# A third PSUM bank for the attention scores, and fewer exponentials in PSUM

## The chip, the cores and the metric

One core of a Trainium2 chip runs the whole kernel. The metric is the device time of one execution in microseconds; the median of several runs is compared. TensorE (PE) multiplies, VectorE (DVE) and ScalarE (ACT) read and write both SBUF and the eight PSUM banks, GpSimd (POOL) works on SBUF, and SyncE (SP) issues the transfers. Each engine executes its own instructions strictly in the order in which the program issues them; between engines, semaphores order producers, consumers and the reuse of buffers.

## The reference

A transformer block with adaptive layer norm. Sequence 2048, width 512, 32 query heads and 8 key/value heads of 128, the last 512 keys of a cache, then a gated feed-forward layer of width 1792. All inputs are f32.

```python
mod = (silu(c) @ w_mod).reshape(1, 6, 1, 512)          # shift, scale and gate, twice
h = layernorm(x) * (1 + ca) + sa
q = h @ wq                                             # (2048, 32 x 128)
p = softmax(q @ k^T * 128**-0.5)                       # over 512 keys, per head
x = x + ga * ((p @ v) @ wo)
h = layernorm(x) * (1 + cb) + sb
x = x + gb * ((gelu(h @ w_gate) * (h @ w_up)) @ w_down)
```

## The kernel before

Every f32 product is made of three f16 products: each operand is split into a high half and a residual, `high` and `low`, and `mm3` (lines 87 to 91) issues low x high, high x high and high x low into one PSUM bank. With f16 halves, a group of three matmuls of 128x128 by 512 columns is the unit of PE work everywhere.

The attention is cut into 128 **units**: one head and one block of 512 queries. A unit has four **slots**, each of 128 queries against all 512 keys, so there are 512 slots, counted by `t`; slot `t` belongs to unit `t // 4`. The main loop (lines 1564 to 1609) issues for each slot, in this order:

- `scores(t)` (line 979): one `mm3` group into a bank called `ps`;
- `peak(t)` (line 988): on DVE, the negated row maximum `nm` of that bank;
- the DVE halves of whatever projection or value product ended in the slot before (`split_post`, line 746: ACT writes the high half, DVE the residual; tiles `qt`, `ot`, and some weights `w`, `k`);
- the reciprocals `rr` of two slots' row sums (line 1002), each second slot;
- `low(t - 3)` (line 1014): on DVE, the f16 residual of the probabilities, from the exponentials `ee`, the factor `rr` and the high half; then, on SP, a transposing DMA of the slot's high half and residual into the tile `pt`;
- `expo(t)` (line 993): on ACT, the exponential of the scores into `ee` with its row sum;
- `high(t - 2)` (line 1009): on ACT, the high half of the probabilities;
- up to three groups from the queue `work` (line 1507, `pop`), with the steps that follow them. In the stretch of the change these are the next unit's query projection (`q_plain`, line 921: four groups into a bank `pq`) and the value product of the unit two before (`pv_tasks`, line 935: four groups into `po`). A value product reads all four transposed slots of its unit. From slot 30 on, groups of the output projection (`y_tasks`, line 948, bank `py`) join them.

So in slots 12 to 29 a unit has 36 matmuls, and the fourth slot of a unit pops nothing; later a unit has 48.

POOL meanwhile scales and splits weights and keys (lines 155 to 163), and makes the sums and differences of activations (line 582) for a seven-product scheme that replaces `q_plain` from unit 12 on (`q_items`, line 898; first issued near slot 42).

PSUM has eight banks under three names. `s` (two banks) holds scores, in turn. `acc` (five banks) is handed out in turn to everything that accumulates: `pq`, `po`, `py`, small reductions (`pst`, `prow`). `qa` (one bank) is used at the start for matmuls that keep PE running and for one small product (slots 2 to 9), and again by `q_items`. A tile that takes a bank waits until the last reader of the bank's former tile is done.

The table `PSE` (line 56) names the slots whose exponentials `ee` go to a PSUM bank, and which one: 13 slots take an `acc` bank and 5 the `qa` bank. All other slots write `ee` to one of six SBUF buffers (`tmp`, line 75). In both cases `high` and `low` read `ee` from where it lies; `low` also reads the high half, which is in SBUF, and writes to SBUF.

## Time and profile before

| what | value |
|---|---|
| runs, median (lowest to highest of 3) | 1733.12 us (1732.55 to 1733.29) |
| the profiled execution | 1734.19 us |
| its span, first to last instruction | 1732.4 us |
| PE busy | 1711.2 us, 99% of the span |
| DVE busy | 1425.8 us, 82% |
| ACT busy | 1254.3 us, 72% |
| POOL busy | 1093.3 us, 63% |
| `ee` on ACT, 512 times | 349.6 us, mean 683 ns |
| residual `low` on DVE, 512 times | 454.1 us, mean 887 ns |
| transposing DMA, 512 times | 3.5 us from issue to landing, median |

A busy PE in this table is not a PE at its peak: matmuls overlap, and a matmul's row is longer than the distance to the next one. Times in the timelines count from the start of the span. An instruction's row also overlaps the next row of its engine a little, so the time that it holds its engine is read from start to start. In a timeline, a bracket gives the idle time of the engine before the row and what ended it. In the groups the names stand as `out<-in`, and line 91 is that of `mm3`, whatever called it.

### The profile page before, as it was taken

To read this page: it belongs to the slowest core of one execution; us is meant where nothing else is said; L and a number is where in the kernel's file an instruction comes from. 1 tells how busy PE (TensorE), PEld (TensorE's weight loads), DVE (VectorE), ACT (ScalarE), POOL (GpSimd) and SP (SyncE) were. 2 spreads that over 40 slices of the span, in tenths; PEclk is the share of its full clock that TensorE was granted. 3 is DMA by queue.
4 is the path that set the end of the run, shared out by engine and by line. 5 is a ranking of instruction groups with operands and counts; after the bars stand their busy time and mean duration, and the time that the engine had idled before them with its cause. 6 is when DMAs were issued, how large, how long until landed. Compare 5 with 4: busy or idle time off the path is not lost.

```text
span 1732.4 us, 26343 instructions
## 1 busy us (share of the span) xinstructions
PE 1711.2 (99%) x8012; PEld 787.1 (45%) x8012; DVE 1425.8 (82%) x2476; ACT 1254.3 (72%) x2819; POOL 1093.3 (63%) x1328
## 2 busy tenths in 40 slices
PE   7999999999999999999999999999999999999998
PEld 5444444444444444444444444444444444444444
DVE  7888898988888899888888888888896788676666
ACT  6988788888888777897787777787785354455442
POOL 4879778777788884655665755747760345735424
PEclk9999999999999999999999999999999999999999
DMA  7999999999999998999999999999997556355353
GB/s 234 218 208 210 214 214 205 225 205 220 211 229 222 206 210 181 219 207 224 198 232 219 206 231 208 203 218 221 229 227 164 163 145 196 118 164 174 96 157 104
DMA packets 693454, 343.51 MB, mean 198 GB/s; under 512 B 579136, under 2 KB 602688, under 8 KB 693312
## 3 DMA queue, kind: packets, MB, share of 16 engines
q1 hardware_dynamic: 693024, 341.30, 85.4%
q8 instruction: 63, 1.03, 0.3%
q14 instruction: 79, 0.65, 0.1%
q10 hardware_dynamic: 288, 0.52, 0.1%
HBM read 137.50 MB, written 63.70 MB: 116 GB/s over the span
## 4 chain that ended last, share of the span: by engine, by line
PE 86%; DVE 5%; ACT 4%; POOL 2%; DMA 2%; issue 1%; SPq 0%; POOLq 0%; DVEq 0%; ACTq 0%
PE py L91 18%; PE po L91 17%; PE ps L91 16%; PE fa L91 8%; PE qa L91 8%; PE fc L91 4%; PE qc L91 4%; PE ya L91 3%; PE fb L91 2%; PE qb L91 2%; PE yc L91 2%; ACT ee L999 1%; DVE p L1016 1%; DVE nm L990 1%; ACT p L1011 1%
## 5 line engine op out<-in xcount | busy, mean ns | idle before, releaser
L999 ACT ACTIVATE ee<-ps,nm 128x512 f32<-128x512 f32 x512 | 349.6, 683 | 184.2 <-DVE nm L990 181.0
L1016 DVE SCALAR_TENSOR_TENSOR p<-ee,rr,p 128x512 f16<-128x512 f32 x512 | 454.1, 887 | 8.1 <-ACT p L1011 7.5
L990 DVE TENSOR_REDUCE nm<-ps 128x1 f32<-128x512 f32 x512 | 350.3, 684 | 105.7 <-PE ps L91 102.9
L91 PE MATMUL ps<-k,qt 128*128 128x512 f16 x1536 | 414.9, 379 | 3.8 <-ACT ee L999 2.5
L1011 ACT ACTIVATE p<-ee,rr 128x512 f16<-128x512 f32 x512 | 363.9, 711 | 21.9 <-DMA pt<-p 11.6
L91 PE MATMUL po<-pt,v 128*128 128x512 f16 x1536 | 372.9, 379 | 2.8 <-DVE kmax L184 1.0
L91 PE MATMUL py<-wo,ot 128*128 128x512 f16 x1536 | 371.3, 379 | 0.0
L91 PEld LDWEIGHTS <-w 128*128 128x128 f16 x2184 | 214.0, 98 | 259.7 <-issue 2.7
L91 PEld LDWEIGHTS <-v 128*128 128x128 f16 x1536 | 149.9, 98 | 185.1 <-issue 5.1
L91 PEld LDWEIGHTS <-ot 128*128 128x128 f16 x1536 | 150.3, 98 | 181.2
L91 PEld LDWEIGHTS <-qt 128*128 128x128 f16 x1536 | 145.8, 98 | 174.8 <-issue 3.3
L1320 POOL TENSOR_TENSOR fg<-fg 128x512 f32<-128x512 f32 x48 | 63.0, 1312 | 147.0 <-DVE fg L1294 144.2
L748 DVE SCALAR_TENSOR_TENSOR ot<-po,ot 128x512 f16<-128x512 f32 x128 | 87.8, 686 | 37.7 <-ACT ot L747 37.3
L1304 ACT ACTIVATE at<-fg 128x512 f16<-128x512 f32 x92 | 56.3, 626 | 80.1 <-DVE fg L1294 61.7
L999 ACT ACTIVATION_READ_ACCUMULATOR ee<-ps,nm 128x1 f32 x512 | 100.1, 195 | 0.0
L960 DVE SCALAR_TENSOR_TENSOR acc<-py,ysc,acc 128x512 f32<-128x512 f32 x128 | 94.7, 740 | 5.3 <-PE py L91 5.3
L91 PE MATMUL qa<-t,w 128*128 128x512 f16 x348 | 84.9, 379 | 0.0
L236 POOL TENSOR_TENSOR lw<-lw,half__86 128x1 f32<-128x1 f32 x39 | 25.0, 641 | 91.0 <-DVE lw L186 91.0
L91 PE MATMUL fa<-t,w 128*128 128x512 f16 x336 | 81.7, 379 | 0.1
L747 ACT ACTIVATE ot<-po 128x512 f16<-128x512 f32 x128 | 73.9, 577 | 5.0 <-PE po L91 5.0
L403 POOL TENSOR_TENSOR rs<-rs,nhalf 128x1 f32<-128x1 f32 x32 | 18.7, 586 | 92.9 <-DVE rs L397 90.0
L91 PEld LDWEIGHTS <-wo 128*128 128x128 f16 x504 | 49.3, 98 | 60.6 <-issue 1.3
(243 smaller groups left out, 2821.9 us busy)
## 6 DMA issues: line engine op xcount, KB each, us to landing
w<-kept SPq DMA_DIRECT2D x123, 256.0 KB, 3.3
wo<-kept SPq DMA_DIRECT2D x72, 256.0 KB, 3.3
kept<-stage SPq DMA_DIRECT2D x67, 256.0 KB, 3.2
raw<-in_wo SPq DMA_DIRECT2D x56, 256.0 KB, 3.2
kept<-w SPq DMA_DIRECT2D x39, 256.0 KB, 3.3
rw<-in_wq SPq DMA_DIRECT2D x38, 256.0 KB, 3.1
hs<-hf SPq DMA_DIRECT2D x32, 256.0 KB, 2.8
pt<-p SPq DMA_TRANSPOSE x512, 3.5
```

Of the source, the lines that this page charges most:

```text
L91: nc.tensor.matmul(ps, a, b, start=first and n == 0, stop=last and n == 2, skip_group_check=chain)
L236: nc.gpsimd.tensor_tensor(out, out, half_, op=ALU.pow)
L403: nc.gpsimd.tensor_tensor(st["rs"], st["rs"], nhalf, op=ALU.pow)
L747: nc.scalar.activation(t[:, 0, :], src, AF.Copy, scale=scale)
L748: return lambda: nc.vector.scalar_tensor_tensor(t[:, 1, :], src, scale, t[:, 0, :], op0=ALU.mult, op1=ALU.subtract)
L960: nc.vector.scalar_tensor_tensor(acc[ti], st["p"], by, acc[ti], op0=ALU.mult, op1=ALU.add)
L990: nc.vector.tensor_reduce(nm, E[t]["ps"], axis=AX.X, op=ALU.max, negate=True)
L999: nc.scalar.activation(e, E[t]["ps"], AF.Exp, bias=E[t]["nm"], scale=1.0, accum_out=sm[:, t % 2:t % 2 + 1])
L1011: nc.scalar.activation(p16[:, 0, :], E[t]["e"], AF.Copy, scale=E[t]["r"])
L1016: nc.vector.scalar_tensor_tensor(p16[:, 1, :], E[t]["e"], E[t]["r"], p16[:, 0, :], op0=ALU.mult, op1=ALU.subtract)
L1304: nc.scalar.activation(t[:, 0, :], g, AF.Copy)
L1320: nc.gpsimd.tensor_tensor(g[o], g[a], g[b], op=ALU.subtract)
```

## The change

```diff
-PSE = dict.fromkeys((5, 7, 8, 9, 14, 18, 19, 21, 22, 23, 25, 26, 27), "acc") | dict.fromkeys((11, 15, 20, 24, 28), "qa")
+PSE = dict.fromkeys((5, 6, 10, 14, 18, 19, 20, 22, 23, 24, 26, 27, 28), "acc")
...
     def scores(t):
...
-        ps = bank("s", "ps", 2)
+        ps = bank("qa", "ps", 1) if 12 <= t < 40 and t % 3 == 2 else bank("s", "ps", 2)
```

Two things change. The scores of slots 14, 17, 20, 23, 26, 29, 32, 35 and 38 go into the `qa` bank; the slots between them share the two `s` banks in turn as before, so that from slot 14 to about slot 40 a score bank is taken again three slots later and not two. And the `qa` bank is no longer used for exponentials: the table names 13 slots, all with `acc` banks. Against the table before, slots 7, 8, 9, 11, 15, 21 and 25 go from PSUM to SBUF, slots 6 and 10 from SBUF to PSUM, and slots 20, 24 and 28 from the `qa` bank to an `acc` bank. No instruction is added or removed, and the order of instructions on each engine stays as it was.

## The prediction

> **What bounds the kernel now.** I read the page first, then busy time by stretch, then the chain of waits inside the stretch that the diff touches, then the timelines of that stretch engine by engine.

> ```profile
> span 1732.4 us, 26343 instructions
> ...
> PE 86%; DVE 5%; ACT 4%; POOL 2%; DMA 2%; issue 1%; SPq 0%; POOLq 0%; DVEq 0%; ACTq 0%
> ...
> pt<-p SPq DMA_TRANSPOSE x512, 3.5
> ```

> TensorE holds 86% of the chain. Slots 5 to 40 fall between 39 and 125 us. Busy time there, in three stretches:

> ```profile
> 25.00:52.80 27.80, 26.60 (x146) 14.62 (x147) 23.41 (x49) 22.89 (x56) 15.88 (x25) 1.00 0.80 183
> 52.80:97.00 44.20, 40.21 (x178) 17.30 (x176) 38.74 (x71) 40.12 (x99) 34.72 (x44) 0.96 1.01 215
> 97.00:130.00 33.00, 32.94 (x156) 15.04 (x157) 27.78 (x52) 26.70 (x63) 24.20 (x35) 1.00 0.93 209
> ```

> Columns: stretch, length, then busy time of PE, weight loads, DVE, ACT, POOL, then the granted clock. After 97 us PE idles 0.06 us in 33. In the 44.2 us before, PE idles 4, ACT 4.1 and DVE 5.5. So whatever the change does must be done before 97 us, and a shift of that moment goes through to the end. The chain of waits there begins and ends so:

> ```profile
> 52.11 0.68 PE ps L91 x3
> ...
> 97.06 1.46 PE po L91 x6
> ```

> Every piece between these two lines is DVE, ACT or issue time; PE does not appear once. PE's own waits there: in the first line those of score groups for exponentials (total, times, longest), then rows of the timeline (in brackets: idle before the row and what ended it):

> ```profile
> PE ps L91 <- ACT ee L999: 2.4, 3, 1.9
> ```
> ```profile
> 60.22 1.46 PE L91 MATMUL po<-pt,v 128*128 128x512 f16 x6 [0.65 <-DVE ysc L234]
> ...
> 82.82 0.95 PE L91 MATMUL ps<-k,qt 128*128 128x512 f16 x3 [1.86 <-ACT ee L999]
> 83.57 2.77 PE L91 MATMUL pq<-y,w 128*128 128x512 f16 x6
> ...
> 93.05 2.10 PE L91 MATMUL pq<-b,w 128*128 128x512 f16 x9
> ...
> 97.06 1.46 PE L91 MATMUL po<-pt,v 128*128 128x512 f16 x6 [0.61 <-DVE nm L990]
> ```

> The three score groups (slots 20, 23, 24; the last at 82.82) found their bank still read by the exponential of two slots before. The wait at 97.06 is put down to `nm`, which the value product does not need. What it needs is the transposed tile of slot 23, last of its unit:

> ```profile
> 91.53 0.75 DVE L748 SCALAR_TENSOR_TENSOR qt<-pq,qsc,qt 128x512 f16<-128x512 f32 x1 [0.24 <-ACT qt L747]
> 92.20 0.15 DVE L1007 RECIPROCAL rr<-rr 128x2 f32<-128x2 f32 x1
> 92.27 0.73 DVE L1016 SCALAR_TENSOR_TENSOR p<-ee,rr,p 128x512 f16<-128x512 f32 x1
> ```
> ```profile
> 93.06 1.23 SPq L1020 DMA_TRANSPOSE pt<-p  x1
> ```

> The residual ends at 93.00, SP issues the transpose at 93.06, and with the page's median of 3.5 us it lands near 96.6; I take the landing as the releaser. So before 97 us the pace is that of DVE and ACT handing slots to one another, and PE waits for slot 23.

> **The third score bank.** No instruction is added. Nine score groups change bank; each score group of slots 14 to 40 then waits for the exponential three slots back, not two. That takes away the 2.4 us of PE idling (1.86 of it at 82.82), and the slow matmuls behind the longest (rows at 82.82 and 83.57). What is late next?

> ```profile
> 81.53 0.75 DVE L748 SCALAR_TENSOR_TENSOR qt<-pq,qsc,qt 128x512 f16<-128x512 f32 x1 [0.98 <-ACT qt L747]
> ```

> Slot 24 opens unit 6, whose queries' low half this row writes until 82.28; the third score matmul reads it. So this group gains at most 0.4 us. The projection behind it (83.57) takes the accumulator bank five tiles back, the last unit's projection, which the same row reads: it cannot start before 82.28 either. PE's next value product needs slot 19, whose residual ended at 83.00, and after it comes the wait of 97.06. PE time won here is handed back in front of these. I price the bank at 0, covered by the landing of slot 23. Bounds: -0.4 (if the residuals follow the scores a little) to 0.

> **The exponentials.** 18 PSUM destinations become 13: slots 7, 8, 9, 11, 15, 21 and 25 go to SBUF, 6 and 10 to PSUM; 20, 24 and 28 only change from the q bank to the accumulators. Two instructions per moved slot change their source: ACT's `high` and DVE's `low`.

> ```profile
> 56.51 0.67 ACT L1011 ACTIVATE p<-ee,rr 128x512 f16<-128x512 f32 x1
> 57.08 0.59 ACT L152 ACTIVATE gate<-prow 128x512 f32<-128x512 f32 x1
> ...
> 59.69 0.71 ACT L1011 ACTIVATE p<-ee,rr 128x512 f16<-128x512 f32 x1
> 60.31 0.62 ACT L219 ACTIVATE junk<-raw 128x512 f16<-128x512 f32 x1
> ```

> Slot 9 (PSUM) holds ACT 0.57 us to the next start, slot 10 (SBUF) 0.62. On the chain are slots 9, 11, 15 and 21, and slot 10 the other way: (4 - 1) x 0.05 = +0.15 us.

> DVE's residual is the larger term:

> ```profile
> 54.16 0.73 DVE L1016 SCALAR_TENSOR_TENSOR p<-ee,rr,p 128x512 f16<-128x512 f32 x1
> ...
> 56.09 0.74 DVE L1016 SCALAR_TENSOR_TENSOR p<-ee,rr,p 128x512 f16<-128x512 f32 x1
> 57.70 0.69 DVE L192 TENSOR_REDUCE gam<-gate 128x1 f32<-128x512 f32 x1 [0.87 <-ACT gate L152]
> ...
> 63.84 0.73 DVE L1016 SCALAR_TENSOR_TENSOR p<-ee,rr,p 128x512 f16<-128x512 f32 x1
> 64.49 0.68 DVE L990 TENSOR_REDUCE nm<-ps 128x1 f32<-128x512 f32 x1
> 65.48 0.69 DVE L748 SCALAR_TENSOR_TENSOR ot<-po,ot 128x512 f16<-128x512 f32 x1 [0.30 <-ACT ot L747]
> ...
> 74.33 1.42 DVE L1016 SCALAR_TENSOR_TENSOR p<-ee,rr,p 128x512 f16<-128x512 f32 x1
> ...
> 86.59 0.72 DVE L1016 SCALAR_TENSOR_TENSOR p<-ee,rr,p 128x512 f16<-128x512 f32 x1
> 87.95 0.69 DVE L990 TENSOR_REDUCE nm<-ps 128x1 f32<-128x512 f32 x1 [0.64 <-PE ps L91]
> ```
> ```profile
> 50.64 0.92 POOL L159 TENSOR_SCALAR w<-rw 128x512 f16<-128x512 f32 x1
> ...
> 53.56 0.62 POOL L159 TENSOR_SCALAR w<-rw 128x512 f16<-128x512 f32 x1
> 54.27 1.15 POOL L160 TENSOR_TENSOR w<-rw,w 128x512 f16<-128x512 f32 x1
> ...
> 63.35 1.27 POOL L582 TENSOR_TENSOR u<-cb,u 128x512 f32<-128x512 f32 x1
> ...
> 73.94 1.26 POOL L657 TENSOR_TENSOR wor<-wor,gs 128x512 f32<-128x512 f32 x1
> ```

> Slot 16 (74.33, SBUF) started inside a POOL pass that ended at 75.20 and itself ended at 75.75, 0.55 later, after 1.42 us. Slot 11 (63.84, PSUM) lay inside a POOL pass too and took 0.73. Bounds for a moved slot: 0 (POOL idle or behind) to +0.7.

> [...]

> Slot by slot. *Slot 7*: slot 6, now read from PSUM, no longer slows the POOL pass at 50.64 (0.92 against 0.62), so POOL runs 0.3 us earlier and its add of 54.27 spans 53.97 to 55.12. Slot 7's residual at 54.16 falls inside: it ends at 55.12 + 0.55 = 55.67, not 54.89, **+0.78**. The next maximum, its exponential, ACT's `gate` (57.08) and DVE's wait of 0.87 us for it all queue behind, so it stays. *Slot 8* (56.09): taken as blocked too, but DVE waits 0.87 us for the gate behind it, and that wait covers up to 0.7: 0. *Slots 9, 15 and 25*: POOL's timeline shows it idle or in one-column operations there: 0. *Slot 11*: inside the pass 63.35 to 64.62, ends 65.17 in place of 64.57; the maximum behind it then runs 65.09 to 65.70, past the 65.48 at which the next row starts today after waiting 0.30 for ACT: **+0.22** on the chain. *Slot 21* (86.59): blocked by at most 0.7, with the 0.64 behind it (87.95) as cover; if the third bank removes that wait, the next cover is DVE's wait for ACT at 91.53: 0. Sum: 0.78 + 0.15 + 0.22 = 1.15, say **+1.2 us** on slot 23's residual, its landing, 97.06, and the end.

> The profiled execution took 1734.19 us (1.8 around its span); the median of the runs is 1733.12, 1.07 lower. So 1735.4 for a profile and **1734.3 us** for the median. A measurement of this kernel tells 0.2%, 3.5 us, from no change; the forecast lies within.

> **The rivals.** *The score banks were the limit (faster).* If slot 23 follows the scores, the 2.4 us go, and with them the slow clock:

> ```profile
> 81.00:82.80 1.80, 0.00 (x0) 0.10 (x1) 1.27 (x3) 1.80 (x5) 1.72 (x3) 1.00 0.23 50
> 82.80:86.20 3.40, 3.38 (x10) 1.27 (x10) 3.40 (x6) 2.44 (x6) 3.22 (x4) 0.58 1.17 307
> ```

> After 1.86 us of idling the granted clock averaged 0.58 over 3.4 us, and six matmuls took 2.77 us (83.57) against 1.46 (60.22): 3.4 x (1 - 1.46 / 2.77) = 1.6 us lost. Time: 1733.1 - 2.4 - 1.6 = 1729.1. For it: the waits are there. Against it: the chain holds no PE piece, and ACT is busy 40.1 us of 44.2.

> *The wait ahead of slot 29's value product lowers the clock (slower).* That wait (97.06) grows. The projection at 93.05 needs the bank that DVE reads until 92.28. By the forecast this is 93.5, so PE comes 0.45 us later to the wait and the landing 1.2 us later: 0.61 + 0.75 = 1.4 us of idling. If slot 8 (up to 0.7) and half of slot 21's (0.3) are not covered either, it passes 1.86, the length after which the clock fell. That is the point from which it decides: 1.6 us at the low clock, with nothing behind to absorb them. Time: 1733.1 + 1.2 + 1.0 + 1.6 = 1736.9. [...]

> *Slot 7 slips ahead of POOL's add.* It starts at 54.16, POOL's pass before ended at 54.18; if POOL is not earlier, slot 7 costs 0 and the sum is 0.4: 1733.5.

> **How the numbers follow.** Forecast 0.43, slot 7 ahead 0.16, low clock 0.27, score banks 0.14. Same: 0.43 + 0.16 = 0.59; slower 0.27; faster 0.14. The range leaves out the score banks and the far end of the low clock. It begins at 1731.6, 1.5 below no change: two of DVE's contended residuals (0.7 each, as at 74.33) may miss POOL once everything is shifted. It ends at 1737.4, 0.5 above the low clock's time for a later landing. The forecast's own: 1733.3 (slot 7 costing 0, and a little) to 1735.2 (slot 8 uncovered as well).

> **What would show it.** Right: no `ps` waits on `ee` between 72 and 83 us; in their place waits of the projection and value groups; slots 7 and 11 with residuals over 1 us; the PE wait that now ends at 97.06 ends near 98.2; no idling after it. Wrong: that wait ends before 96, or PE idles after it, or the residuals stay at 0.73.

## The result, and the profile after

| | before | changed |
|---|---|---|
| median of 13 runs (lowest to highest), same chip | 1732.94 us (1731.75 to 1734.70) | 1736.84 us (1734.82 to 1737.74) |
| ratio to before, 95% interval | | 1.0021, 1.0014 to 1.0029 |
| profiled execution; its span | 1734.19; 1732.4 us | 1737.74; 1736.0 us |

The change costs 3.9 us, 0.21%. The interval lies above 1, so the kernel is slower, by about the 0.2% that the prediction took as the least that can be told. The forecast was +1.2 us and "same"; the time lies inside its range, near the end, and the rival of the low clock named 1736.9.

The difference is made before slot 30. "Shift" below is how much later a slot's residual starts than in the kernel before, each trace counted from its own slot 0. The residuals of slots 0 and 30 in DVE's timeline, before and changed:

```profile
36.45 0.84 DVE L1016 SCALAR_TENSOR_TENSOR p<-ee,rr,p 128x512 f16<-128x512 f32 x1
...
107.70 0.73 DVE L1016 SCALAR_TENSOR_TENSOR p<-ee,rr,p 128x512 f16<-128x512 f32 x1
```
```profile
36.72 0.83 DVE L1016 SCALAR_TENSOR_TENSOR p<-ee,rr,p 128x512 f16<-128x512 f32 x1
...
111.87 0.74 DVE L1016 SCALAR_TENSOR_TENSOR p<-ee,rr,p 128x512 f16<-128x512 f32 x1
```

(111.87 - 107.70) - (36.72 - 36.45) = 3.90 us. At slot 21 the shift is only 1.18, at slot 24 it is 3.38, and from slot 27 on 3.89. So 1.2 us come from the exponentials, as forecast, 2.2 us from something between slots 21 and 24, and 0.5 us from something between slots 24 and 27. Busy time by stretch (columns as in the prediction) says what kind of thing:

```profile
25.00:52.80 27.80, 26.32 (x145) 14.52 (x146) 23.47 (x51) 22.88 (x55) 15.58 (x25) 1.00 0.79 188
52.80:97.00 44.20, 37.86 (x165) 15.85 (x163) 36.81 (x65) 37.19 (x89) 36.03 (x43) 0.92 0.94 206
97.00:130.00 33.00, 32.08 (x152) 14.55 (x151) 28.04 (x54) 27.59 (x67) 20.27 (x31) 1.00 0.89 191
```

In the middle stretch DVE and ACT now idle 7.4 and 7.0 us (before 5.5 and 4.1), PE idles 6.3 (before 4.0), and the clock is 0.92 (before 0.96). None of the three works more; all three wait more. The two longest of PE's waits between 45 and 130 us (total, times, longest), and PE's timeline around them:

```profile
PE pq L91 <- DVE ot L748: 3.6, 2, 2.7
PE ps L91 <- ACT qt L747: 1.5, 1, 1.5
```
```profile
80.75 0.81 PE L91 MATMUL ps<-k,qt 128*128 128x512 f16 x3
83.02 0.60 PE L91 MATMUL ps<-k,qt 128*128 128x512 f16 x2 [1.46 <-ACT qt L747]
83.80 0.39 PE L91 MATMUL ps<-k,qt 128*128 128x512 f16 x1 [0.18 <-DVE qt L748]
86.85 2.72 PE L91 MATMUL pq<-y,w 128*128 128x512 f16 x6 [2.65 <-DVE ot L748]
89.36 1.48 PE L91 MATMUL pq<-b,w 128*128 128x512 f16 x3
90.64 1.25 PE L91 MATMUL ps<-k,qt 128*128 128x512 f16 x3
...
98.00 2.10 PE L91 MATMUL pq<-b,w 128*128 128x512 f16 x9 [0.92 <-DVE ot L748]
...
101.23 1.46 PE L91 MATMUL po<-pt,v 128*128 128x512 f16 x6
```

The waits of score groups for exponentials are gone, as the third bank promised. Slot 24's scores (83.02, 83.80) now wait for its queries, 1.46 and 0.18 us. Behind them stands a wait that the kernel before did not have: slot 24's projection (86.85) waits 2.65 us for DVE's `ot`. Its six matmuls then take 2.72 us, where six take 1.46 at full clock. A second wait of the same kind, 0.92 us, stands before slot 28's projection (98.00). The granted clock, by stretches cut where it changes:

```profile
81.28:84.69 3.41, 1.28 (x5) 0.23 (x4) 2.43 (x6) 3.38 (x9) 3.23 (x4) 1.00 1.22 316
84.69:88.11 3.42, 1.26 (x4) 0.42 (x4) 3.42 (x7) 2.46 (x7) 3.24 (x4) 0.50 0.92 221
88.11:91.52 3.41, 3.41 (x10) 1.17 (x9) 0.97 (x2) 2.82 (x8) 3.24 (x4) 0.50 0.83 186
```

The clock is at 0.50 for 6.83 us; in the profile of before it was so for 3.41 us. In the last of these stretches DVE works 0.97 us of 3.41: now the slow matmuls set the pace. DVE's rows: the residual of slot 19, `ot` of the value product issued in slot 21, the residual of slot 21, the maximum behind it, and the residual of slot 23:

```profile
83.73 0.73 DVE L1016 SCALAR_TENSOR_TENSOR p<-ee,rr,p 128x512 f16<-128x512 f32 x1
...
86.12 0.67 DVE L748 SCALAR_TENSOR_TENSOR ot<-po,ot 128x512 f16<-128x512 f32 x1
...
88.04 1.04 DVE L1016 SCALAR_TENSOR_TENSOR p<-ee,rr,p 128x512 f16<-128x512 f32 x1
91.93 0.69 DVE L990 TENSOR_REDUCE nm<-ps 128x1 f32<-128x512 f32 x1 [2.85 <-PE ps L91]
...
95.94 0.72 DVE L1016 SCALAR_TENSOR_TENSOR p<-ee,rr,p 128x512 f16<-128x512 f32 x1
```

`ot` ends at 86.79 and PE starts at 86.85. Slot 25's scores come late (90.64), its maximum waits 2.85 us for them, and slot 23's residual (95.94) is 3.40 late.

**Which bank the projection takes.** This `ot` is the last reader of slot 21's value product (`po`). The bank numbers of the compiled programs:

```
accumulator bank of    ee slot 19   po slot 21   ee slot 24   pq slot 24
before                      3            0         q bank          3
changed                     1            2            1            2
table only (e1)             1            2            1            2
changed, 24 in SBUF (e3)    1            2         SBUF            1
```

Before, slot 24's projection took the bank of slot 19's exponential, whose last reader was done at 83.00. In the changed kernel slot 24's own exponential, now an accumulator tile and issued just ahead of that projection, takes it. The projection gets that of slot 21's value product, free at 86.79, 2.3 us after slot 19's residual ended (84.46). Slot 28's projection moves in the same way: before and in e3 it takes the bank of slot 23's exponential, in the changed kernel and in e1 that of slot 25's value product.

### The profile page after: what moved, and what is told of

Same layout as the page of the kernel before. It is cut to its first block, busy times and chain, and to the rows that moved or that the text cites. A ratio compares the mean times of both kernels' runs of the same rounds, so it can differ in the third digit from the quotient of the medians.

```text
span 1736.0 us, 26342 instructions
## 1 busy us (share of the span) xinstructions
PE 1712.2 (99%) x8012; PEld 787.1 (45%) x8012; DVE 1426.7 (82%) x2476; ACT 1254.8 (72%) x2819; POOL 1092.1 (63%) x1328
## 4 chain that ended last, share of the span: by engine, by line
PE 86%; DVE 5%; ACT 3%; POOL 2%; DMA 2%; issue 2%; SPq 0%; POOLq 0%; DVEq 0%; ACTq 0%
PE py L91 18%; PE ps L91 16%; PE po L91 16%; PE fa L91 8%; PE qa L91 8%; PE fc L91 4%; PE qc L91 4%; PE ya L91 3%; PE fb L91 2%; PE qb L91 2%; PE yc L91 2%; DVE p L1016 1%; PE pq L91 1%; DVE nm L990 1%; ACT ee L999 1%
## 5 line engine op out<-in xcount | busy, mean ns | idle before, releaser
L999 ACT ACTIVATE ee<-ps,nm 128x512 f32<-128x512 f32 x512 | 349.5, 683 | 187.6 <-DVE nm L990 182.6
L1016 DVE SCALAR_TENSOR_TENSOR p<-ee,rr,p 128x512 f16<-128x512 f32 x512 | 456.1, 891 | 6.4 <-ACT p L1011 5.8
L990 DVE TENSOR_REDUCE nm<-ps 128x1 f32<-128x512 f32 x512 | 350.0, 684 | 108.2 <-PE ps L91 106.0
L91 PE MATMUL ps<-k,qt 128*128 128x512 f16 x1536 | 415.1, 379 | 3.0 <-ACT qt L747 1.5
L1011 ACT ACTIVATE p<-ee,rr 128x512 f16<-128x512 f32 x512 | 364.1, 711 | 20.8 <-DVE rr L1007 10.6
L91 PE MATMUL po<-pt,v 128*128 128x512 f16 x1536 | 372.9, 379 | 2.6 <-DMA pt<-p 1.2
L91 PE MATMUL py<-wo,ot 128*128 128x512 f16 x1536 | 371.3, 379 | 0.0
L91 PEld LDWEIGHTS <-w 128*128 128x128 f16 x2184 | 213.9, 98 | 263.4 <-issue 6.7
L91 PEld LDWEIGHTS <-v 128*128 128x128 f16 x1536 | 150.0, 98 | 185.0 <-issue 4.8
L91 PEld LDWEIGHTS <-ot 128*128 128x128 f16 x1536 | 150.2, 98 | 181.3
L91 PEld LDWEIGHTS <-qt 128*128 128x128 f16 x1536 | 145.9, 98 | 174.5 <-ACT qt L747 3.2
L748 DVE SCALAR_TENSOR_TENSOR ot<-po,ot 128x512 f16<-128x512 f32 x128 | 87.7, 685 | 39.3 <-ACT ot L747 39.1
L999 ACT ACTIVATION_READ_ACCUMULATOR ee<-ps,nm 128x1 f32 x512 | 100.1, 195 | 0.0
L91 PE MATMUL qa<-t,w 128*128 128x512 f16 x348 | 84.9, 379 | 0.0
L91 PE MATMUL fa<-t,w 128*128 128x512 f16 x336 | 81.6, 379 | 0.1
L747 ACT ACTIVATE ot<-po 128x512 f16<-128x512 f32 x128 | 73.8, 576 | 5.0 <-PE po L91 5.0
L91 PEld LDWEIGHTS <-wo 128*128 128x128 f16 x504 | 49.3, 98 | 59.8 <-issue 0.6
```

The costliest lines, as they stand in the source:

```text
L91: nc.tensor.matmul(ps, a, b, start=first and n == 0, stop=last and n == 2, skip_group_check=chain)
L747: nc.scalar.activation(t[:, 0, :], src, AF.Copy, scale=scale)
L748: return lambda: nc.vector.scalar_tensor_tensor(t[:, 1, :], src, scale, t[:, 0, :], op0=ALU.mult, op1=ALU.subtract)
L990: nc.vector.tensor_reduce(nm, E[t]["ps"], axis=AX.X, op=ALU.max, negate=True)
L999: nc.scalar.activation(e, E[t]["ps"], AF.Exp, bias=E[t]["nm"], scale=1.0, accum_out=sm[:, t % 2:t % 2 + 1])
L1011: nc.scalar.activation(p16[:, 0, :], E[t]["e"], AF.Copy, scale=E[t]["r"])
```

## The experiments

Medians of 11 runs each. e1 to e4 share one chip and their runs of before (1733.30), as do e5 to e8 (1733.24), and e9 and e10 (1732.85). "Full clock" counts the executions whose mean granted clock is 1.000 to three digits, so without a low period of 3.4 us (which takes off 0.001). An execution that is not counted need not have had one near slot 24: the clock also falls at the very end (in the trace of before it is 0.50 from 1732.00 us on), and e3's profiled execution, at 1.00 from 80 to 97 us, has a mean of 0.999.

| | median | ratio, 95% | shift, slot 21 | shift, slot 30 | full clock |
|---|---|---|---|---|---|
| changed | 1736.84 | 1.0021, 1.0014-1.0029 | +1.18 | +3.90 | 0 of 13 |
| e1 table only | 1736.16 | 1.0014, 1.0006-1.0023 | +1.19 | +3.22 | 0 of 11 |
| e2 bank only | 1733.54 | 1.0004, 0.9996-1.0013 | +1.01 | +1.12 | 4 of 11 |
| e3 24 in SBUF | 1734.43 | 1.0006, 0.9997-1.0015 | +1.20 | +1.35 | 7 of 11 |
| e4 wait filled | 1733.77 | 1.0002, 0.9993-1.0011 | +1.21 | +1.75 | 8 of 11 |
| e5 6 in SBUF | 1735.57 | 1.0014, 1.0005-1.0024 | +0.44 | +2.16 | 0 of 11 |
| e6 6, 24 in SBUF | 1734.19 | 1.0007, 0.9998-1.0016 | +0.43 | +0.62 | 7 of 11 |
| e7 15 in PSUM | 1735.66 | 1.0011, 1.0002-1.0020 | +0.77 | +4.05 | 0 of 11 |
| e8 before, 16, 17 in PSUM | 1732.41 | 0.9995, 0.9986-1.0004 | -0.42 | -0.43 | 11 of 11 |
| e9 half filled | 1734.84 | 1.0008, 1.0000-1.0017 | +1.21 | +1.75 | 8 of 11 |
| e10 2 fills | 1736.57 | 1.0022, 1.0013-1.0031 | +1.20 | +3.25 | 0 of 11 |

Shifts are those of one profiled execution each. After slot 30, waits of PE that differ between executions move a trace by up to 1.6 us (e4: +1.75 at slot 30, +0.16 at slot 511), so a shift and a median may be that far apart. An interval is about 3 us wide: the medians alone do not tell e2, e3, e4 and e6 from before, nor e1, e5, e7 and e10 from the changed kernel. Where a cause is placed at a slot, below, it is the shifts and waits that place it.

**e1: the table alone.** Two score banks as before.

```diff
-PSE = {5, 7, 8, 9, 14, 18, 19, 21, 22, 23, 25, 26, 27: "acc"; 11, 15, 20, 24, 28: "qa"}
+PSE = {5, 6, 10, 14, 18, 19, 20, 22, 23, 24, 26, 27, 28: "acc"}
```

> The changed table of exponentials with the two score banks of before. Theory A (the loss is a wait of slot 24's projection for the accumulator bank of the value product before it, 2.65 us in the changed kernel, and the low clock behind it; the table makes that wait, the score bank has no part in it): +3.9 us against before, as the changed kernel, within 0.6; the projection after slot 24 starts near 86.9 and waits for DVE's ot. Rival B (the third score bank itself delays PE): at most +1.2 us, the blocked residuals of slots 7 and 16 alone. Rival C (the third bank gains what its waits cost before): over +4.5 us.

Median +2.9 us, under the 3.3 to 4.5 of theory A; near slot 24 the trace has one low period and not two. The wait is the one that theory A names. PE's timeline of e1 has the old wait for an exponential and the new one for the bank, one behind the other:

```profile
85.15 0.81 PE L91 MATMUL ps<-k,qt 128*128 128x512 f16 x3 [1.86 <-ACT ee L999]
87.70 1.53 PE L91 MATMUL pq<-y,w 128*128 128x512 f16 x4 [1.75 <-DVE ot L748]
```

The wait for `ot` does not need the third score bank. The table makes it.

**e2: the third score bank alone.** The q bank's five exponentials must leave it; they go to SBUF, and the other 13 stay as before.

```diff
-11, 15, 20, 24, 28: "qa"
+                                    # left out of PSE: SBUF
...
+ps = bank("qa", "ps", 1) if 12 <= t < 40 and t % 3 == 2 else bank("s", "ps", 2)
```

> The third score bank with the accumulator exponentials of before; slots 11, 15, 20, 24 and 28, which lay in the q bank, go to SBUF because that bank now holds scores. Theory A: the projection after slot 24 takes the bank of slot 19's exponential as before, so no wait over 1 us stands there; the score waits of 2.4 us are gone; slots 11 and 20 are slowed by POOL at most 0.5 each. Sum between 0 and +1.0 us, taken +0.4. Rival B: +2.5 us or more. Rival C (score banks were the limit): -2.4 us or better.

Not to be told from before. PE's timeline of e2:

```profile
83.37 1.47 PE L91 MATMUL pq<-y,w 128*128 128x512 f16 x6 [0.33 <-DVE p L1016]
```

Slot 24's projection waits 0.33 us, for slot 19's residual (`p`), and runs at full clock. The shift of 1 us at slot 21 is that of the residuals which went to SBUF. It falls to 0.80 by slot 24 and is at 1.12 at slot 30, ahead of which slot 29's residual takes 1.70 us in place of 1.43. So the third bank by itself, with the waits it removes, gains at most about 0.2 us.

**e3: the changed kernel with slot 24's exponential in SBUF.**

```diff
-PSE = dict.fromkeys((5, 6, 10, 14, 18, 19, 20, 22, 23, 24, 26, 27, 28), "acc")
+PSE = dict.fromkeys((5, 6, 10, 14, 18, 19, 20, 22, 23, 26, 27, 28), "acc")
```

> The changed kernel with slot 24's exponential in SBUF, nothing else: the projection after slot 24 then takes the bank of slot 19's exponential in place of the value product's. Theory A: its wait falls from 2.65 us to under 1, the clock stays up longer, and the end comes at +1.2 us against before (the shift of slots 7 and 16 that stands by slot 21). Rival D (the residuals that POOL blocks make the whole loss): +3.5 to +4.3 us, since not one of them leaves SBUF here.

```profile
84.11 1.47 PE L91 MATMUL pq<-y,w 128*128 128x512 f16 x6 [0.33 <-DVE p L1016]
...
94.14 2.10 PE L91 MATMUL pq<-b,w 128*128 128x512 f16 x9 [0.33 <-DVE p L1016]
```

One number out of the table, and in PE's timeline the 2.65 us are 0.33, with slot 19's residual as releaser again; the shift at slot 30 falls from 3.90 to 1.35, and the median is 1.1 us above before in place of 3.9. Slot 28's projection (94.14) waits for a residual again as well, 0.33 us, so this one number mends both late banks.

**e4, e9, e10: the changed kernel with the wait filled.** Behind slot 24's scores, dummy matmuls of ones go into the bank that slot 25's scores then overwrite: 10 in e4, 5 in e9, 2 in e10. They keep PE active; the bank that the projection needs comes free no sooner.

```diff
+        if t == 24:
+            E["next"] = bank("s", "ps", 2)             # slot 25 takes this tile
+            for _ in range(10):
+                nc.tensor.matmul(E["next"], ones.to_broadcast([P, P]), ones.to_broadcast([P, 512]), start=True, stop=True)
```

> The changed kernel with ten dummy matmuls in the wait of 2.65 us, into slot 25's score bank, which slot 25 then overwrites. The wait for the bank stays. If the low clock behind the wait costs on its own, the 13 matmuls that took 0.43 us in place of 0.22 run at full clock: slot 25's scores come up to 2.7 us earlier and the end is +1.2 to +2.2 us. If the wait alone makes the loss, +3.9 us.

> The changed kernel with 5 dummy matmuls of ones behind slot 24's scores, in place of the 10 of the kernel that filled the whole wait; they go into the bank that slot 25's scores then overwrite. Theory (grid): in the ten traces so far every change of the granted clock falls on a grid of 3.413 us that does not start with the kernel, and the clock falls at the end of a grid period in which PE idled 2.07 us or more, not after 1.82 or less (one exception, 1.56 near 23 us). Five matmuls take 1.2 us, so no 3.41 us around the wait holds more than about 1.75 us of idling, wherever the grid lies: PE still waits about 1.4 us for the accumulator bank, the clock stays at 1.00, and slot 30's residual is 1.75 us later than before, as with the whole wait filled; median 1733.8 to 1734.4. Rival (length of a wait): a gap of over a microsecond behind the idling for slot 24's queries lowers the clock all the same; then 3.4 us at 0.50 and slot 30 at +2.5 to +3.9, median 1735 to 1737.

> As the run with 5 dummy matmuls, but with 2 (0.5 us). PE then waits about 2.1 us in one piece, more than the 1.86 after which the clock fell in the kernel before. Theory (grid): what counts is the idling inside one grid period, not the wait. The clock falls only if a period ends between about 86.0 and 86.6 us, where it holds the whole wait (2.07 or more); in five of six positions of the grid each period holds at most 2.0 and the clock stays at 1.00, with slot 30 at +1.75 and the median near 1734. The trace's own periods must agree: low if one of them holds 2.07 or more, high if all hold 1.82 or less. Rival (length of a wait): a wait of over 1.86 us lowers the clock in each execution: 3.4 us at 0.50, slot 30 at +2.5 or more, median 1735 or more.

PE's timelines of e4 (with rows for nine of its ten fills), e9 and e10, and under them the busy times of e4, then of e10 ahead of and in its low period:

```profile
83.79 2.35 PE L990 MATMUL ps<-ones 128*128 128x512 bf16 x9
86.35 1.45 PE L91 MATMUL pq<-y,w 128*128 128x512 f16 x6 [0.22 <-DVE ot L748]
```
```profile
83.78 1.25 PE L990 MATMUL ps<-ones 128*128 128x512 bf16 x5
86.33 1.46 PE L91 MATMUL pq<-y,w 128*128 128x512 f16 x6 [1.30 <-DVE ot L748]
...
95.32 2.10 PE L91 MATMUL pq<-b,w 128*128 128x512 f16 x9 [1.06 <-DVE ot L748]
```
```profile
83.57 0.59 PE L990 MATMUL ps<-ones 128*128 128x512 bf16 x2
86.12 2.09 PE L91 MATMUL pq<-y,w 128*128 128x512 f16 x6 [1.96 <-DVE ot L748]
```
```profile
80.00:97.00 17.00, 14.09 (x62) 5.86 (x62) 15.36 (x26) 15.54 (x38) 14.70 (x14) 1.00 1.03 219
```
```profile
83.38:86.79 3.41, 1.35 (x7) 0.50 (x6) 3.41 (x6) 2.46 (x8) 3.23 (x4) 1.00 1.08 223
86.79:90.21 3.42, 3.42 (x10) 1.22 (x9) 1.56 (x3) 3.42 (x9) 3.25 (x4) 0.50 0.82 187
```

In all three the projection starts when `ot` ends. With 10 or 5 fills the clock stays at 1.00 and the shift is +1.75; with none it is +3.90. So in that execution the low clock cost 2.15 us, and the late banks by themselves about 0.55 (1.75 - 1.20). Slot 24's late bank has next to no part in this: in e4 the shift is still 1.23 at slot 24 and 1.27 at slot 25. It grows to 1.75 by slot 27. In between stands the wait of slot 28's projection (95.32 in e9), and slot 29's scores, issued behind that projection, come late for their maximum. In DVE's timeline of e4:

```profile
98.12 0.69 DVE L994 TENSOR_REDUCE nm<-ps 128x1 f32<-128x512 f32 x1 [0.66 <-PE ps L91]
```

That this second bank costs the half microsecond is read from these traces; no run changes it alone. Between e10 and e9 the only difference is three dummy matmuls: work added makes the kernel 1.7 us faster (1736.57 and 1734.84).

e4's shift came out as expected; its median is 0.5 us over before, below the 1.2 to 2.2. e9 came out as its first theory says in shift and clock; its median lies 2.0 us over before where 0.5 to 1.1 was expected. e10 did not: the theory of grid periods expected the clock to hold in five of six executions, and none of 11 is at full clock (eight have a mean of 0.998). The rival, that a wait of this length lowers it each time, fits.

**e5, e6, e7: one slot back at a time.**

```diff
 after: (5, 6, 10, 14, 18, 19, 20, 22, 23, 24, 26, 27, 28)
 e5:    (5,    10, 14, 18, 19, 20, 22, 23, 24, 26, 27, 28)
 e6:    (5,    10, 14, 18, 19, 20, 22, 23,     26, 27, 28)
 e7:    (5, 6, 10, 14, 15, 18, 19, 20, 22, 23, 24, 26, 27, 28)
```

> The changed kernel with slot 6's exponential in SBUF as before, nothing else; slot 24's projection still takes the value product's bank. If slot 7's residual is blocked because slot 6, read from PSUM, lets POOL's add start 0.3 us earlier: slot 6's residual takes 0.92 again, POOL's add starts after slot 7's residual, which takes 0.73 to 0.9 in place of 1.48, and all behind it comes 0.7 us earlier; the end at +3.1 us against before in place of +3.9. If slot 7 is blocked wherever it lies in SBUF: no change, +3.9.

> Both mends in one: slots 6 and 24 in SBUF, else the changed kernel. If the three terms add (slot 7 0.8, slot 16 0.4, the bank wait with its low clock 2.7): +0.4 us against before at slot 30, only slot 16's longer residual being left. If one of them covers another: +1.2 or more.

> The changed kernel with slot 15's exponential also in PSUM. If slot 15's residual, read from SBUF, holds up POOL's one-column operation by 0.43 us (0.62 against 0.19) and so moves POOL's multiply onto slot 16's residual: that operation takes 0.19 again, slot 16's residual about 1.42 in place of 1.82, and the shift at slot 17 is +0.8 in place of +1.2 us. If slot 11 makes slot 16 longer: slot 16 stays at 1.82 and the shift at +1.2. The wait for the bank stays in either case: the end at +3.5 or +3.9 us.

Slot 7's residual in DVE's timeline of the changed kernel and of e5, then POOL's rows beside it in the same order:

```profile
54.43 1.48 DVE L1016 SCALAR_TENSOR_TENSOR p<-ee,rr,p 128x512 f16<-128x512 f32 x1
```
```profile
53.59 0.73 DVE L1016 SCALAR_TENSOR_TENSOR p<-ee,rr,p 128x512 f16<-128x512 f32 x1
```
```profile
50.89 0.62 POOL L159 TENSOR_SCALAR w<-rw 128x512 f16<-128x512 f32 x1
...
54.21 1.16 POOL L160 TENSOR_TENSOR w<-rw,w 128x512 f16<-128x512 f32 x1
55.34 1.13 POOL L163 TENSOR_SCALAR raw<-raw,ksc 128x512 f32<-128x512 f32 x1
...
57.26 1.59 POOL L160 TENSOR_TENSOR k<-raw,k 128x512 f16<-128x512 f32 x1
```
```profile
53.69 1.66 POOL L160 TENSOR_TENSOR w<-rw,w 128x512 f16<-128x512 f32 x1
```

With slot 6 back in SBUF, POOL is late again. Slot 7 starts first, takes 0.73, and POOL's add pays instead (1.66 in place of 1.16). The shift at slot 21 falls by 0.74 us.

Slot 16 in DVE's timeline, changed kernel and e7, and POOL's rows of both:

```profile
75.41 1.82 DVE L1016 SCALAR_TENSOR_TENSOR p<-ee,rr,p 128x512 f16<-128x512 f32 x1
```
```profile
74.88 1.42 DVE L1016 SCALAR_TENSOR_TENSOR p<-ee,rr,p 128x512 f16<-128x512 f32 x1
```
```profile
73.42 0.62 POOL L240 TENSOR_SCALAR lw<-lw 128x1 f32<-128x1 f32 x1
...
75.42 1.27 POOL L657 TENSOR_TENSOR wor<-wor,gs 128x512 f32<-128x512 f32 x1
```
```profile
72.92 0.19 POOL L240 TENSOR_SCALAR lw<-lw 128x1 f32<-128x1 f32 x1
...
74.48 1.27 POOL L657 TENSOR_TENSOR wor<-wor,gs 128x512 f32<-128x512 f32 x1
```

Slot 15's residual, moved to SBUF, takes its usual 0.73, but a one-column POOL operation beside it takes 0.62 in place of 0.19. POOL's next big pass then begins with slot 16's residual and not 0.4 us ahead of it, and slot 16 pays for the whole pass. With 15 in PSUM the 0.40 us are gone.

Both medians stay 2.3 to 2.4 us above before, since slot 24 is still in an accumulator bank (PE waits 2.65 us there in both). The size missed: e5's shift was 2.16 where about 3.1 was expected, and e7 gave nothing back by slot 30. The granted clock accounts for it. In e5, then e7, the stretches behind the wait:

```profile
84.66:88.07 3.41, 2.81 (x7) 0.98 (x7) 2.83 (x5) 3.38 (x10) 3.24 (x4) 0.50 1.01 277
88.07:91.49 3.42, 3.42 (x17) 1.57 (x16) 2.07 (x3) 2.59 (x8) 3.42 (x4) 1.00 1.00 258
```
```profile
85.09:88.50 3.41, 2.58 (x7) 0.92 (x7) 3.06 (x6) 3.16 (x9) 3.24 (x4) 0.50 0.84 211
88.50:91.91 3.41, 3.41 (x10) 1.21 (x9) 0.67 (x2) 1.51 (x4) 3.33 (x4) 0.50 1.01 260
```

The same wait brought one low period in e5 and two in e7. What they cost follows the matmul time that falls into them. PE is busy at the low clock for 2.81 us in e5, 3.42 in e10, 4.67 in the changed kernel and 5.99 in e7. From slot 21 to slot 30 the shift grows by 0.54 in e4 and e9, which have no low period, and by 1.72, 2.05, 2.72 and 3.28 in these four: 0.54, and a little under half of that matmul time. e6, with neither slot 6 nor 24 in PSUM, has no low period there and the smallest shift of the changed kernels. In the shifts the two causes add (3.90 - 0.74 - 2.55 = 0.61; measured 0.62); the medians of e3 and e6 (+1.1 and +1.0) are too close to show it.

**e8: the kernel before, with slots 16 and 17 in PSUM in place of 15.** Two score banks.

```diff
-14, ..., 18: "acc"; 11, 15, 20, 24, 28: "qa"
+14, ..., 17, 18: "acc"; 11, 16, 20, 24, 28: "qa"
```

> A version meant to beat both: the kernel before with slot 16 in place of 15 in the q bank and slot 17 added to the accumulators, so that the two residuals of 1.42 and 1.55 us that POOL blocks come from PSUM. The third score bank is left out. If the chain before 97 us runs through these two residuals: about 0.73 us each, slot 23's residual 0.7 us earlier (the rest goes into ACT's own work), the end at -0.7 us, -0.04%. If ACT alone sets the pace there: 0.

DVE's timeline of e8, slot 17 and the row behind it:

```profile
75.54 0.73 DVE L1016 SCALAR_TENSOR_TENSOR p<-ee,rr,p 128x512 f16<-128x512 f32 x1
76.61 1.28 DVE L748 SCALAR_TENSOR_TENSOR w<-rw,wsc,w 128x512 f16<-128x512 f32 x1 [0.34 <-ACT w L747]
```

Slots 16 and 17 take 0.74 and 0.73 us (before 1.42 and 1.55), 1.5 us less on DVE, but only 0.43 reach slot 30: DVE then waits for ACT, and its `w` residual meets POOL's pass instead (1.28). The median is 0.8 us lower, with an interval that holds 1. No version here is shown to beat the kernel before.

## Why the prediction was partly right

*Slot 7, +0.78: right.* Its own chain of reasons held: slot 6 in PSUM, POOL's conversion 0.62, its add 0.3 us earlier, slot 7 inside it, 1.48 us. The shift is +0.79 at slot 9, and e5 takes it away.

*Slot 8, blocked but covered: right in cost, wrong in kind.* It started ahead of POOL's add (the row at 57.26) and took 0.73 us; the add took 1.59 in place of 1.16.

*Slot 11, +0.22 on the chain: wrong.* The residual was blocked, but by 0.37 us (1.10 in place of 0.73) and not the 0.60 counted on, since POOL's pass began earlier against it. The shift at slot 12 was still +0.78: DVE's wait of 0.30 us for ACT behind it is gone, and covered it.

*ACT's +0.15: wrong.* Slots 9 and 10 began +0.79 and +0.75 late, slots 12 to 15 +0.78 to +0.81. About 0.02 reached the chain.

*Slot 15, 0 because POOL is in one-column operations: wrong*, +0.40 through slot 16, as e7 shows. That the sum of 1.15 met the measured 1.18 is luck: two terms too many (0.22 + 0.15) and one missing (0.40).

*Slot 21, hidden: right.* It took 1.04, and DVE waited behind it.

*The third score bank, 0: right* for the bank itself: in e2 it gained at most about 0.2 us, and the changed kernel, which has it, is not faster than e1, which does not. Slot 24's scores did gain nothing to speak of, for the reason given, the queries. The rival that the score banks were the limit falls.

**The step that failed** is "20, 24 and 28 only change from the q bank to the accumulators", costed at nothing, and with it "the projection behind it takes the accumulator bank five tiles back, the last unit's projection". The banks are not handed out in strict turn. An accumulator tile more ahead of slot 24's projection put this one on the bank of the last value product. The wait is 2.65 us; by itself it adds next to nothing, but the low clock that it brings adds 2.15 us. The same shift of banks makes slot 28's projection wait 0.92 us, which adds about 0.5 (e4, e9; both are gone in e3).

The rival of the low clock was right in kind, idling that lowers the clock with nothing behind to absorb it, and its 1736.9 stands beside 1736.84. Its place was wrong: slot 24's projection, not slot 29's value product (101.23, no wait), and the idling came from a bank and not from a late transpose. That the times meet is luck: its sum was 1.2 + 1.0 + 1.6, the runs show 1.2 + 2.15 + 0.55. And the sign named for the forecast, that wait ending near 98.2 with no idling after it, did not come: the wait is gone.

## What to carry to other kernels

Where several kinds of tile share PSUM banks, a tile that moves into the shared group shifts the bank of each tile behind it: look up, for each large consumer behind the move and not for the next one alone, which bank it takes now and who reads that last. An idle gap of PE must be costed with the clock that it takes down, here 0.42 to 0.47 of the matmul time that fell into the low periods (2.81 to 5.99 us, in e5, e10, the changed kernel and e7); a gap that hid behind other engines may stop hiding when the slow matmuls become the pace, as they did here from 88.11 us on (DVE worked 0.97 us of 3.41). And a DVE operation that came to read SBUF beside POOL delayed here either itself (slot 7, 1.48 us in place of 0.73) or POOL (the add beside slot 8, 1.59 in place of 1.16), so that the bill can come one slot later, as that of slot 15 came at slot 16 (1.82 in place of 1.42).

## What the runs showed of the hardware

Counted by grid periods, the clock fell in this stretch behind periods with 2.06 (e10), 2.08 (before), 2.13 (changed), 2.23 (e1) and 2.42 us (e5, e7) of idling and not behind 1.82 (e1), and it rose again behind periods with 0.60 (e5) or none (before, changed, e1, e10), not behind 0.83 (e7) or 2.16 (changed). Outside it the expectation of e9 names one exception (1.56 near 23 us). But e10 does not fit the count by periods alone, by which five of six executions were expected to hold the clock: none of 11 is at full clock. What fixes one low period or two, and so perhaps much of the spread of the changed kernel's runs, stays open.

**A blocked residual ended 0.54 to 0.55 us after POOL's pass.** In the changed kernel slot 7 ended at 55.91, 0.54 after the add's end at 55.37; slot 11 at 66.00, 0.55 after 65.45; slot 16 at 77.23, 0.54 after 76.69, though its row begins 0.01 us ahead of POOL's. A whole residual takes 0.73. Of slot 7's residual and POOL's add, the one that started later was held up: the residual in the changed kernel (54.43 against 54.21; it took 1.48), the add in e5 (53.69 against 53.59; 1.66 in place of 1.16). So slot 7 cost 0.75 us. A one-column POOL operation was held up as well: 0.62 us beside slot 15's residual in the changed kernel, against 0.19 in e7.
